# Clearing an output in quarter blocks, spread over the loads of a recurrence and expert kernel

## Chip, cores and metric

One core of a Trainium2 chip. The metric is the device time of one execution in microseconds (us); lower is better.

## What is computed

Two stages, the second on the output of the first:

```python
# x, f_logit: (4, 5056, 256) float32; lower_bound: (256,)
f = lower_bound + (1 - lower_bound) * sigmoid(f_logit)
h[t] = f[t] * h[t-1] + (1 - f[t]) * x[t]          # along the 5056 steps, y[:, t] = h[t]

x = y.reshape(20224, 256)                         # N = 20224 tokens, D = 256, E = 8, F = 1024
logits = x @ w_gate
expert = argmax(logits); gate_w = softmax(logits)[expert]
out = zeros((20224, 256))
for e in range(8):
    tok = the up to 80 tokens of expert e with the largest gate_w
    out[tok] = gate_w[tok] * (relu(x[tok] @ w1[e]) @ w2[e])
```

At most 640 of the 20224 rows of the output are other than zero, and the kernel has to write all of them: 20.7 MB of zeros.

## The kernel before

The sequence is cut into 40 units (`n_unit`): 10 groups of 512 steps (the last one of 448) by 4 sequences. A unit is worked in a pipeline. `load` (lines 195 to 202) brings f and x of a unit from DRAM to two tiles of 128 rows (112 in the last group), with four buffers each. `gate` (L206, ScalarE) makes the sigmoid in place, `enter` (L210, GpSimd) multiplies it into x, `to_channels` (L217, TensorE) transposes both, the sigmoid to `sp` and the product to `up`, eight transposes each; `decay` (L228, ScalarE) writes the factors to `h_all`, and `scan` (L234, VectorE) runs the recurrence there. `logits` (L246, TensorE) multiplies the unit by the gate weights into `lg`. With each finished group, copies, transposes and small VectorE work pick the candidates of each expert (L253 to L351).

The loop (lines 385 to 402) runs n from -3 to 39 and issues in each step the load of unit n + 3, the gate and product of unit n + 2, the transposes of n + 1, the scan of n and the logits of n - 1. All loads, all clears of the output and all expert weights are DMAs issued by SyncE (SP), in the order of the code; an instruction there that waits holds up all that stand behind it. A load waits until its buffer is free, which is when TensorE has transposed the unit four before. Apart from that, SyncE's DMAs share eight completion counters in turn, so each waits until the one eight before it has landed.

Zeros: GpSimd fills a small tile (L173), and ScalarE's queue copies it several times over to a block in DRAM, `z_dram`, 128 rows of 2048 numbers, 1.05 MB (L175, in `setup`). A clear (L146) is a DMA of this block to 8 of the 158 rows that each of 128 stripes of the output has; 20 clears cover it, the last of 6 rows. Before the loop's last load five have gone out; where they go out is written in the loop (L396: behind the logits of the steps n = -3, 5, 13, 21, 29 and 37), behind the first three weights (L445, eleven), and in the experts behind w1 of expert 2 and w2 of expert 1 (L652, the other three):

```python
            if n % 8 == 5:
                clear_some(1)
...
    clear_some(11)
...
                if e == 0 and not again:
                    clear_some(len(zeros))
```

After the loop come the rest of the choice, the selection (L485 to L556, VectorE for the most part), and the eight experts: `gather` (L583, three engines copy 80 columns), `hidden` (L601, TensorE), `relu` (L609), `result` (L616, TensorE), `finish` (L622) and `scatter` (L625, an indirect DMA of GpSimd, which may not pass a clear). Weights come in halves of 0.524 MB (L433 for w1, L437 for w2) to seven buffers, whose place in memory the loop's tiles hold until the loop is through.

Of the kernel before, what the change touches and what calls it, by code (L numbers as in the profile page):

```python
# [17 lines left out]
P = 128  # L18
# [5 lines left out]
def kernel(  # L24
# [11 lines left out]
    nc = tc.nc  # L36
    B, S, D = x.shape
    E, _, F = w1.shape
# [3 lines left out]
    R = 4  # L42
    G = P * R
    n_grp = (S + G - 1) // G
    n_unit = n_grp * B
# [93 lines left out]
    z_dram = dram.tile([P, ZR * D], F32, name="z_dram")  # L139
    out_z = out.rearrange("(p k) d -> p (k d)", p=P)  # L140
    clears = range(0, N // P, ZR)
    zeros = list(clears)

    def clear(k):
        n = min(ZR, N // P - k) * D
        nc.sync.dma_start(out=out_z[:, ds(k * D, n)], in_=z_dram[:, :n])  # L146

    def clear_some(m):
        for k in zeros[:m]:
            clear(k)  # L150
        del zeros[:m]

    with tc.tile_pool(name="ld", bufs=4) as ld, \
         tc.tile_pool(name="gsm", bufs=1) as gsm, \
# [57 lines left out]
        def to_channels(n, src, dst, pool, tag):  # L212
            k = run(n // B)
            for o in range(DC):
                ps = pool.tile([P, G], F32, name=tag, tag=tag)
                for r in range(R):
                    nc.tensor.transpose(ps[:, ds(r * k, k)], src[n][:, r, ds(o * P, P)],  # L217
                                        ident[:k, :k])
                dst[n, o] = ps[:, :R * k]
            del src[n]  # L220
# [29 lines left out]
        def aside(g):  # L250
            k = run(g)
            lss[g] = gsm.tile([P, B * P], F32, name="ls", tag="ls")[:, :B * k]
            nc.scalar.copy(lss[g].rearrange("p (b t) -> p b t", b=B), lgs.pop(g)[:, :, :k])  # L253
# [111 lines left out]
        def unit(f, m):  # L365
            if 0 <= m < n_unit:
                f(m)


        AHEAD = 3  # L370
        of_group, of_batch = [], []

        def chosen(g):
            choice(g)
            if g in batches:
                of_batch.extend(work(*batches[g]))

        def some_of(jobs, k):
            while jobs and k:
                for f in jobs.pop(0):  # L380
                    f()
                k -= 1

        setup()
        for n in range(-AHEAD, n_unit):
            unit(load, n + AHEAD)
            unit(gate, n + 2)
            unit(enter, n + 2)
            unit(lambda m: to_channels(m, sts, sps, pss, "sp"), n + 1)
            unit(lambda m: to_channels(m, uts, ups, psu, "up"), n + 1)  # L390
            unit(decay, n + 1)
            unit(scan, n)
            some_of(of_group, 1)
            some_of(of_batch, 1 if n < n_unit - 2 else 2)
            unit(logits, n - 1)
            if n % 8 == 5:  # L396
                clear_some(1)
            if n > 0 and n % B == 0:
                g = n // B - 1
                of_group += [[lambda g=g: aside(g)], [lambda g=g: shifted(g)],  # L400
                             [lambda g=g: chosen(g)]]
# [40 lines left out]
    w_sb = {}  # L442
    for key in order[:3]:
        w_sb[key] = weights(*key)
    clear_some(11)  # L445


    def tokens(pool, at, ids):
# [115 lines left out]
    def experts(again):  # L564
        with tc.tile_pool(name="xp", bufs=2) as xp, \
             tc.tile_pool(name="mp", bufs=2) as mp, \
             tc.tile_pool(name="psd", bufs=1, space=PSUM) as psd, \
             tc.tile_pool(name="psh", bufs=4, space=PSUM) as psh, \
             tc.tile_pool(name="psy", bufs=2, space=PSUM) as psy:
            w = {} if again else w_sb  # L570
            late = list(order if again else order[3:])
            X, XT, HID, Y = {}, {}, {}, {}


            def gather(e):
                X[e] = xp.tile([P, DC, K], F32, name="xe", tag="xe")
                k = 0
                for engine, copy, n in ways:
                    _, at_tok = nc.values_load_multi_w_load_instructions(
                        trow[ds(e, 1), ds(k, n)], engines=(engine,), min_val=0, max_val=N - 1,  # L580
                        skip_runtime_bounds_check_because="token numbers come from iota")
                    for j, v in enumerate(at_tok):
                        copy(X[e][:, :, ds(k + j, 1)], h_all[:, :, ds(v, 1)])  # L583
                    k += n

            def scaled(e):
                XT[e] = mp.tile([P, DC, K], F32, name="xt", tag="xt")
                x_e = X.pop(e)
                for o in range(DC):
                    nc.vector.tensor_scalar_mul(XT[e][:, o], x_e[:, o], omlb[:, ds(o, 1)])  # L590

            def hidden(e):
                HID[e] = mp.tile([P, FC, K], F32, name="hid", tag="hid")
                xt = XT.pop(e)
                halves = w.pop((1, e))
                ps = []
                for i in range(2):
                    h_ps = psh.tile([P, CH, K], F32, name="h_ps", tag="h_ps")
                    for c in range(CH):
                        for o in range(DC):  # L600
                            nc.tensor.matmul(h_ps[:, c], halves[i][:, o, ds(c * P, P)], xt[:, o],  # L601
                                             start=o == 0, stop=o == DC - 1,
                                             skip_group_check=True)
                    ps.append(h_ps)
                return ps

            def relu(e, ps):
                for i in range(2):
                    nc.scalar.activation(HID[e][:, ds(i * CH, CH)], ps[i], ACT.Relu)  # L609

            def result(e):
                y_ps = psy.tile([K, D], F32, name="y_ps", tag="y_ps")
                halves = w.pop((2, e))
                hid = HID.pop(e)
                for c in range(FC):
                    nc.tensor.matmul(y_ps, hid[:, c], halves[c // CH][:, c % CH],  # L616
                                     start=c == 0, stop=c == FC - 1)
                return y_ps

            def finish(e, y_ps):  # L620
                Y[e] = mp.tile([K, D], F32, name="y", tag="y", bufs=3)
                nc.vector.tensor_scalar_mul(Y[e], y_ps, gsl[:, ds(e, 1)])  # L622

            def scatter(e):
                nc.gpsimd.indirect_dma_start(  # L625
                    out=out, out_offset=bass.IndirectOffsetOnAxis(ap=goal[:, ds(e, 1)], axis=0),
                    in_=Y.pop(e), in_offset=None, bounds_check=N - 1, oob_is_err=False)

            def more(m):
                for key in late[:m]:  # L630
                    w[key] = weights(*key)
                del late[:m]

            if again:
                more(3)
            for e in range(2):
                gather(e)
                scaled(e)
            ps = hidden(0)
            relu(0, ps)  # L640
            more(1)
            if not again:
                total = psd.tile([1, 4], F32, name="total")
                nc.tensor.matmul(total, ones, doubts[:, :4], start=True, stop=True)
            for e in range(E):
                if e + 2 < E:
                    gather(e + 2)
                if e + 1 < E:
                    ps = hidden(e + 1)
                    relu(e + 1, ps)  # L650
                    more(1)
                if e == 0 and not again:  # L652
                    clear_some(len(zeros))
                y_ps = result(e)
                more(1)
                if e + 2 < E:
                    scaled(e + 2)
                finish(e, y_ps)
                if e > 0:
                    scatter(e - 1)  # L660
                if e == 1 and not again:
                    found = consts.tile([1, 1], F32, name="found")
                    nc.vector.tensor_reduce(found, total, AX.X, ALU.add)
                    nc.vector.tensor_copy(doubt, found)
            scatter(E - 1)

    experts(False)


    unsure = nc.values_load(doubt, min_val=0, max_val=4 * P,  # L670
                            skip_runtime_bounds_check_because="a sum of 4 * P flags")
    with tc.If(unsure > 0):
        with tc.tile_pool(name="all", bufs=1) as sel, \
# [34 lines left out]
            for e in range(E):  # L708
                nc.gpsimd.indirect_dma_start(
                    out=tok[:, ds(e, 1)], out_offset=None, in_=id_list,  # L710
# [7 lines left out]
            for k in clears:  # L718
                clear(k)
        experts(True)  # L720
    hpool.release()

# [30 lines left out]
```

## Time and profile before

| what | us |
|---|---|
| median of three runs | 262.97 (261.96 to 263.56) |
| the profiled execution, its own time | 263.93 |
| its span, first to last instruction | 262.0 |
| busy: TensorE, VectorE, GpSimd, ScalarE | 202.5, 169.4, 135.6, 134.1 |
| loop, selection, experts | to about 150, to about 190, to the end |

Times in the trace are counted from the start of the span. The rows name the engines PE (TensorE), DVE (VectorE), ACT (ScalarE), POOL (GpSimd) and SP (SyncE); SPq and ACTq are the queues on which SyncE and ScalarE issue DMAs, and a row there is the issue, not the transfer. A busy share is an average over stages with different limits: a stage is read from what its last waits were for.

### The profile page before, as it was taken

To read this page: it belongs to the slowest core of one execution; us is meant where nothing else is said; L and a number is where in the kernel's file an instruction comes from. 1 tells how busy PE (TensorE), PEld (TensorE's weight loads), DVE (VectorE), ACT (ScalarE), POOL (GpSimd) and SP (SyncE) were. 2 spreads that over 40 slices of the span, in tenths; PEclk is the share of its full clock that TensorE was granted. 3 is DMA by queue.
4 is the path that set the end of the run, shared out by engine and by line. 5 is a ranking of instruction groups with operands and counts; after the bars stand their busy time and mean duration, and the time that the engine had idled before them with its cause. 6 is when DMAs were issued, how large, how long until landed. Compare 5 with 4: busy or idle time off the path is not lost.

```text
span 262.0 us, 5950 instructions
## 1 busy us (share of the span) xinstructions
PE 202.5 (77%) x1755; PEld 158.2 (60%) x1755; DVE 169.4 (65%) x484; ACT 134.1 (51%) x390; POOL 135.6 (52%) x275
## 2 busy tenths in 40 slices
PE   0519989799999789999899941117099999999990
PEld 0417767576767567776577720016099788888860
DVE  0627877869696779698769687982565066656200
ACT  3037875867777957676977530000445424555100
POOL 2318775868686569694596510300575025664111
PEclk9999999999999999999979995555555699999997
DMA  6699999999999998999999199999994999999700
GB/s 172 249 335 385 383 404 369 386 365 362 381 384 350 356 353 273 362 324 377 316 241 287 65 360 409 345 309 315 324 300 152 393 292 392 390 333 315 233 18 21
DMA packets 58904, 81.09 MB, mean 309 GB/s; under 512 B 2800, under 2 KB 51568, under 8 KB 56432
## 3 DMA queue, kind: packets, MB, share of 16 engines
q1 hardware_dynamic: 57408, 78.91, 89.7%
q10 hardware_dynamic: 1072, 1.06, 1.1%
q0 software_dynamic: 384, 0.66, 0.7%
q8 instruction: 16, 0.26, 0.4%
q14 instruction: 24, 0.20, 0.3%
HBM read 78.91 MB, written 22.41 MB: 387 GB/s over the span
## 4 chain that ended last, share of the span: by engine, by line
PE 52%; DMA 18%; DVE 8%; issue 6%; ACT 6%; POOL 6%; SPq 2%; POOLq 0%; DVEq 0%; ACTq 0%
PE h_ps L601 12%; PE lg L246 10%; PE sp L217 9%; PE up L217 9%; PE y_ps L616 8%; DMA x_t<-in_x_dram 7%; POOL x_t L210 5%; DMA w_sb<-in_moe_w_dram 5%; DMA out_dram<-z_dram 4%; DVE beat L513 3%; ACT h_all L228 3%; DMA z_dram<-zero 3%; DVE h_all L234 2%; PE flat_p L536 2%; PE lt L261 1%
## 5 line engine op out<-in xcount | busy, mean ns | idle before, releaser
L210 POOL TENSOR_TENSOR x_t<-f_t,x_t 128x1024 f32<-128x1024 f32 (+1 forms) x40 | 94.9, 2376 | 47.2 <-DMA x_t<-in_x_dram 21.5
L234 DVE TENSOR_TENSOR_SCAN h_all<-h_all,up 128x512 f32<-128x512 f32 (+1 forms) x80 | 95.5, 1241 | 14.8 <-ACT h_all L228 11.4
L228 ACT ACTIVATE h_all<-sp,nomlb 128x512 f32<-128x512 f32 (+1 forms) x80 | 49.9, 676 | 16.0 <-PE sp L217 15.9
L217 PE MATMUL sp<-ident,f_t 128*128 128x128 f32 (+1 forms) x320 | 45.8, 288 | 15.9 <-ACT h_all L228 8.9
L217 PEld LDWEIGHTS sp<-ident,f_t 128*128 128x128 f32 (+1 forms) x320 | 35.9, 146 | 32.9 <-issue 19.4
L206 ACT ACTIVATE f_t<-f_t 128x1024 f32<-128x1024 f32 (+1 forms) x40 | 42.6, 1064 | 17.7 <-DMA f_t<-in_f_logit_dram 17.7
L217 PE MATMUL up<-ident,x_t 128*128 128x128 f32 (+1 forms) x320 | 44.5, 284 | 4.7 <-POOL x_t L210 3.8
L246 PE MATMUL lg<-h_all,wg 128*32 128x128 f32 (+1 forms) x640 | 43.5, 401 | 5.1 <-ACT ls L253 3.6
L601 PE MATMUL h_ps<-xt,w_sb 128*128 128x80 f32 x256 | 36.4, 311 | 7.2 <-issue 7.0
L217 PEld LDWEIGHTS up<-ident,x_t 128*128 128x128 f32 (+1 forms) x320 | 37.6, 147 | 7.1 <-POOL x_t L210 5.6
L583 ACT COPY xe<-h_all 128x2 f32 x224 | 22.2, 190 | 37.6 <-issue 32.2
L601 PEld LDWEIGHTS h_ps<-xt,w_sb 128*128 128x128 f32 x256 | 36.1, 227 | 8.2 <-issue 7.1
L583 DVE COPY xe<-h_all 128x2 f32 x224 | 26.5, 177 | 14.8 <-issue 14.8
L583 POOL COPY xe<-h_all 128x2 f32 x192 | 24.3, 195 | 15.4 <-DVE goal L475 8.5
L616 PE MATMUL y_ps<-w_sb,hid 128*80 128x256 f32 x128 | 30.3, 393 | 0.0
L246 PEld LDWEIGHTS lg<-h_all,wg 128*32 128x32 f32 x640 | 18.2, 119 | 18.0 <-ACT ls L253 5.5
L625 POOL DMA_INDIRECT out_dram<-y,goal x8 | 7.5, 940 | 33.3 <-DVE y L622 15.6
L616 PEld LDWEIGHTS y_ps<-w_sb,hid 128*80 128x80 f32 x128 | 19.5, 157 | 8.2 <-issue 1.2
L609 ACT ACTIVATE hid<-h_ps 128x320 f32<-128x320 f32 x16 | 7.0, 436 | 22.9 <-PE h_ps L601 19.6
L622 DVE TENSOR_SCALAR y<-y_ps,gsl 80x256 f32<-80x256 f32 x8 | 3.8, 480 | 21.0 <-PE y_ps L616 21.0
L284 DVE TENSOR_REDUCE mx<-lt 128x16 f32<-128x128 f32 (+1 forms) x10 | 2.9, 290 | 12.7 <-PE lt L261 12.6
L286 ACT COPY shift<-lt 128x128 f32<-128x128 f32 (+1 forms) x10 | 2.7, 266 | 15.8 <-DVE lt L285 15.8
(103 smaller groups left out, 102.8 us busy)
## 6 DMA issues: line engine op xcount, KB each, us to landing
out_dram<-z_dram SPq DMA_DIRECT2D x19, 1024.0 KB, 10.0
f_t<-in_f_logit_dram SPq DMA_DIRECT2D x36, 512.0 KB, 7.0
x_t<-in_x_dram SPq DMA_DIRECT2D x36, 512.0 KB, 6.6
w_sb<-in_moe_w_dram SPq DMA_DIRECT2D x32, 512.0 KB, 5.8
f_t<-in_f_logit_dram SPq DMA_DIRECT2D x4, 448.0 KB, 8.2
x_t<-in_x_dram SPq DMA_DIRECT2D x4, 448.0 KB, 7.3
z_dram<-zero ACTq DMA_DIRECT2D x1, 1024.0 KB, 7.5
out_dram<-z_dram SPq DMA_DIRECT2D x1, 768.0 KB, 10.3
```

What stands on the lines that cost most here:

```text
L206: nc.scalar.activation(s_t, s_t, ACT.Sigmoid, scale=-1.0)
L210: nc.gpsimd.tensor_tensor(u_t, sts[n], u_t, ALU.mult)
L217: nc.tensor.transpose(ps[:, ds(r * k, k)], src[n][:, r, ds(o * P, P)], ident[:k, :k])
L228: nc.scalar.activation(columns(n, o), sps.pop((n, o)), ACT.Identity, scale=nomlb[:, ds(o, 1)], bias=1.0)
L234: nc.vector.tensor_tensor_scan(h, h, ups.pop((n, o)), h_all[:, o, ds(spot(n) - 1, 1)] if n >= B else 0.0, ALU.mult, ALU.add)
L246: nc.tensor.matmul(lgs[g][ds(r * LC, LC), b, :k], wg[:, o], columns(n, o)[:, r::R], start=o == 0, stop=o == DC - 1, skip_group_check=True)
L513: nc.vector.tensor_scalar(beat, rivals, vals[:, ds(k, 1)], 0.0, ALU.is_gt, ALU.add, accum_out=rank[:, ds(k, 1)])
L583: copy(X[e][:, :, ds(k + j, 1)], h_all[:, :, ds(v, 1)])
L601: nc.tensor.matmul(h_ps[:, c], halves[i][:, o, ds(c * P, P)], xt[:, o], start=o == 0, stop=o == DC - 1, skip_group_check=True)
L609: nc.scalar.activation(HID[e][:, ds(i * CH, CH)], ps[i], ACT.Relu)
L616: nc.tensor.matmul(y_ps, hid[:, c], halves[c // CH][:, c % CH], start=c == 0, stop=c == FC - 1)
L625: nc.gpsimd.indirect_dma_start(out=out, out_offset=bass.IndirectOffsetOnAxis(ap=goal[:, ds(e, 1)], axis=0), in_=Y.pop(e), in_offset=None, ...
```

## The change

A clear may now take a quarter of the block, 32 of the 128 rows, 0.262 MB, and the list of clears is a list of quarters. In the loop one quarter goes out in each step from n = 8 to 35, and twelve in the step n = 36, in which the last unit's load goes out; the clears that the loop had at n = -3, 5, 13, 21, 29 and 37 are gone. Ten blocks stand for 40 quarters by then. The other ten, in whole blocks, follow the first three weights; the clears among the experts' weights are gone.

```diff
-    zeros = list(clears)
-
-    def clear(k):
+    QP = P // R
+    zeros = [(k, q) for k in clears for q in range(R)]
+
+
+    def clear(k, q=None):
         n = min(ZR, N // P - k) * D
-        nc.sync.dma_start(out=out_z[:, ds(k * D, n)], in_=z_dram[:, :n])
+        rows = slice(0, P) if q is None else ds(q * QP, QP)
+        nc.sync.dma_start(out=out_z[rows, ds(k * D, n)], in_=z_dram[rows, :n])
 
     def clear_some(m):
-        for k in zeros[:m]:
+        for k, q in zeros[:m]:
+            clear(k, q)
+        del zeros[:m]
+
+    def clear_rest():
+        clear_some(len(zeros) % R)
+        for k, _ in zeros[::R]:
             clear(k)
-        del zeros[:m]
+        zeros.clear()
...
-            if n % 8 == 5:
+            if n + AHEAD == n_unit - 1:
+                clear_some(3 * R)
+            elif 2 * B <= n < n_unit - AHEAD:
                 clear_some(1)
...
-    clear_some(11)
+    clear_rest()
...
-                if e == 0 and not again:
-                    clear_some(len(zeros))
```

Only SyncE's order moves. Its first instructions before, where `f_t` and `x_t` are a unit's two loads and `out_dram<-z_dram` is a clear:

```order
L198 DMA f_t<-in_f_logit_dram 128x4x256
L201 DMA x_t<-in_x_dram 128x4x256
L146 DMA out_dram<-z_dram 128x2048
L198 DMA f_t<-in_f_logit_dram 128x4x256
L201 DMA x_t<-in_x_dram 128x4x256
L198 DMA f_t<-in_f_logit_dram 128x4x256
L201 DMA x_t<-in_x_dram 128x4x256
```

The same place now:

```order
L207 DMA f_t<-in_f_logit_dram 128x4x256
L210 DMA x_t<-in_x_dram 128x4x256
L207 DMA f_t<-in_f_logit_dram 128x4x256
L210 DMA x_t<-in_x_dram 128x4x256
L207 DMA f_t<-in_f_logit_dram 128x4x256
L210 DMA x_t<-in_x_dram 128x4x256
```

The clear between the loads of units 0 and 1 is gone; the first zeros now follow the load of unit 11. From there to the last load one quarter stands between the loads of any two units. The end of the loop before, from the load of the last unit to the experts' first weights:

```order
L198 DMA f_t<-in_f_logit_dram 112x4x256
L201 DMA x_t<-in_x_dram 112x4x256
L146 DMA out_dram<-z_dram 128x2048
L433 DMA w_sb<-in_moe_w_dram 128x2x512 x4
L437 DMA w_sb<-in_moe_w_dram 128x4x256 x2
L146 DMA out_dram<-z_dram 128x2048 x11
L433 DMA w_sb<-in_moe_w_dram 128x2x512 x2
L437 DMA w_sb<-in_moe_w_dram 128x4x256 x2
L146 DMA out_dram<-z_dram 128x2048 x2
L146 DMA out_dram<-z_dram 128x1536
L433 DMA w_sb<-in_moe_w_dram 128x2x512 x2
```

The same place now, from the load of the unit before the last:

```order
L207 DMA f_t<-in_f_logit_dram 112x4x256
L210 DMA x_t<-in_x_dram 112x4x256
L149 DMA out_dram<-z_dram 32x2048
L207 DMA f_t<-in_f_logit_dram 112x4x256
L210 DMA x_t<-in_x_dram 112x4x256
L149 DMA out_dram<-z_dram 32x2048 x12
L444 DMA w_sb<-in_moe_w_dram 128x2x512 x4
L448 DMA w_sb<-in_moe_w_dram 128x4x256 x2
L149 DMA out_dram<-z_dram 128x2048 x9
L149 DMA out_dram<-z_dram 128x1536
L444 DMA w_sb<-in_moe_w_dram 128x2x512 x2
```

Between the last load and the first weights stand three blocks' worth of zeros where one was, behind the first weights ten blocks where eleven were, and none further on.

## Rows read from the trace of the kernel before

**Rows 1.** Page, part 2: DMA busy tenths, GB/s in 40 slices

```profile
DMA  6699999999999998999999199999994999999700
...
GB/s 172 249 335 385 383 404 369 386 365 362 381 384 350 356 353 273 362 324 377 316 241 287 65 360 409 345 309 315 324 300 152 393 292 392 390 333 315 233 18 21
```

**Rows 2.** Timeline of SyncE's DMA issues at the start: start us, us, instruction

```profile
1.21 0.49 SPq L201 DMA_DIRECT2D x_t<-in_x_dram  x1
...
9.78 0.61 SPq L146 DMA_DIRECT2D out_dram<-z_dram  x1
...
10.43 0.58 SPq L198 DMA_DIRECT2D f_t<-in_f_logit_dram  x1
```

**Rows 3.** SyncE's waits: who waited for whom, us in total, times, longest

```profile
SPq L146 <- DMA z_dram<-zero: 8.1, 1, 8.1
```

**Rows 4.** Timeline of other engines at the start; brackets: idle time, releaser

```profile
2.28 0.58 ACTq L175 DMA_DIRECT2D z_dram<-zero  x1
...
7.36 2.35 POOL L210 TENSOR_TENSOR x_t<-f_t,x_t 128x1024 f32<-128x1024 f32 x1 [4.92 <-DMA x_t<-in_x_dram]
...
16.67 1.06 ACT L206 ACTIVATE f_t<-f_t 128x1024 f32<-128x1024 f32 x1 [9.85 <-DMA f_t<-in_f_logit_dram]
...
18.47 2.35 POOL L210 TENSOR_TENSOR x_t<-f_t,x_t 128x1024 f32<-128x1024 f32 x1 [8.76 <-DMA x_t<-in_x_dram]
...
20.88 1.97 PE L217 MATMUL up<-ident,x_t 128*128 128x128 f32 x8 [0.56 <-POOL x_t L210]
```

**Rows 5.** Start by stretch: us, busy by engine, then PEclk, DMA share, GB/s

```profile
2.00:4.00 2.00, 0.00 (x0) 0.00 (x0) 0.00 (x0) 1.11 (x1) 0.44 (x2) 1.00 0.76 158
...
4.00:6.00 2.00, 0.00 (x0) 0.00 (x0) 0.24 (x2) 0.42 (x2) 0.00 (x0) 1.00 0.92 286
...
8.00:10.00 2.00, 1.14 (x6) 0.73 (x5) 1.97 (x3) 0.00 (x0) 1.71 (x1) 1.00 0.50 195
```

**Rows 6.** Stretches of the loop, its end and the selection, columns as above

```profile
32.80:45.60 12.80, 12.09 (x130) 8.62 (x128) 9.33 (x13) 8.38 (x13) 8.03 (x4) 1.00 1.07 387
...
112.00:114.00 2.00, 2.00 (x26) 1.26 (x24) 1.93 (x6) 1.39 (x3) 2.00 (x2) 1.00 0.89 218
...
130.00:140.00 10.00, 8.83 (x79) 6.92 (x80) 7.12 (x9) 7.11 (x12) 7.73 (x5) 0.83 1.10 240
...
148.00:150.00 2.00, 2.00 (x20) 1.91 (x19) 0.27 (x1) 1.16 (x2) 0.00 (x0) 1.00 0.00 0
...
166.00:182.00 16.00, 4.83 (x33) 4.78 (x34) 10.75 (x41) 0.00 (x0) 2.83 (x11) 0.50 0.98 319
```

**Rows 7.** Timeline of TensorE in the loop: three lg groups and the last up

```profile
37.56 1.10 PE L246 MATMUL lg<-h_all,wg 128*32 128x128 f32 x16 [0.44 <-ACT ls L253]
...
51.68 1.10 PE L246 MATMUL lg<-h_all,wg 128*32 128x128 f32 x16 [0.52 <-ACT ls L253]
...
64.46 1.11 PE L246 MATMUL lg<-h_all,wg 128*32 128x128 f32 x16 [0.52 <-ACT ls L253]
...
148.68 0.93 PE L217 MATMUL up<-ident,x_t 112*128 112x112 f32 x8
```

**Rows 8.** Timeline at the end of the loop, SyncE and GpSimd

```profile
137.53 0.31 SPq L201 DMA_DIRECT2D x_t<-in_x_dram  x1
...
145.48 2.37 POOL L210 TENSOR_TENSOR x_t<-f_t,x_t 112x1024 f32<-112x1024 f32 x1
...
149.68 1.92 SPq L433 DMA_DIRECT2D w_sb<-in_moe_w_dram  x4
```

**Rows 9.** Tile x_t, issues from 137 to 138 us: issue to landing

```profile
DMA to landing us min/median/max: 7.3/7.3/7.3
```

**Rows 10.** Tile x_t, all issues: issue to landing

```profile
DMA to landing us min/median/max: 4.9/6.7/10.1
```

**Rows 11.** Timeline of TensorE, experts: first and fourth hidden layer

```profile
190.33 7.09 PE L601 MATMUL h_ps<-xt,w_sb 128*128 128x80 f32 x32 [7.01 <-issue]
...
216.70 3.77 PE L601 MATMUL h_ps<-xt,w_sb 128*128 128x80 f32 x32 [0.20 <-DMA w_sb<-in_moe_w_dram]
```

## Prediction

> **What bounds the kernel now.** I read the page's slices first [rows 1]: the DMA engines are near full for most of the span, with two holes: the first two slices (13 us, 172 and 249 GB/s) and the 23rd, 144 to 151 us (65 GB/s). Then SyncE's own timeline and waits [rows 2, 3], since every load, clear and weight goes through that one queue; then what the other engines waited for at the start [rows 4], bandwidth by stretch [rows 5, 6], and the pace of TensorE in the loop [rows 7].
>
> The first hole: SyncE issues the load of x for unit 0 at 1.21 us and nothing more until 9.78, because the next instruction is a clear, and that waits 8.1 us for the block of zeros to be written to DRAM [rows 2, 3]. Unit 1's loads stand behind it. So ScalarE sits idle 9.85 us until f of unit 1 has landed, GpSimd 8.76 us until x has, and TensorE's second group of `up` starts at 20.88 [rows 4]. Meanwhile the DMA engines fall to 195 GB/s in 8 to 10 us [rows 5].
>
> From there TensorE sets the pace. The `lg` group that follows the copy of a finished group's logits starts at 51.68 and at 64.46, four units later: 12.78 us, 3.20 us a unit [rows 7]. A unit's two loads are 2 x 0.524 = 1.049 MB, which at the 387 GB/s of the stretch 32.8 to 45.6 [rows 6] is 2.71 us: under the pace, so loads can run ahead. The four units before that took 51.68 - 37.56 = 14.12 us [rows 7]; a clear of 1.05 MB had gone out among their loads, and 1.3 us were lost.
>
> The last four units' loads are dearer: 112 rows, 0.917 MB a unit, and the stretch 130 to 140 ran at 240 GB/s with a full DMA share [rows 6], 3.82 us a unit. The last x goes out at 137.53 and lands 7.3 us later, at 144.8 [rows 8, 9]; GpSimd takes it at 145.48, TensorE transposes it at 148.68, and the weights, whose buffers lie where the loop's were, go out at 149.68 [rows 7, 8]. That is the second hole: 0 GB/s from 148 to 150 [rows 6], after one clear. Behind it the selection and the experts form one chain to the end.
>
> **The change part by part.**
>
> *No clear before unit 1's loads.* Its wait of 8.1 us and issue go; six loads leave back to back. How much earlier x of unit 1 lands: by 6 us some 2 x 0.158 + 2 x 0.286 = 0.89 MB had moved [rows 5], and that part stays. If the zeros' copy (1.05 MB, issued by ScalarE at 2.28 [rows 4]) goes wholly ahead, 4 x 0.524 + 1.05 = 3.15 MB must move, the remaining 2.26 MB at 387 GB/s in 5.8 us: 11.8. If it comes last, 1.21 MB: 9.1. The landing of the last byte adds between 0 and 1 us: of f and x of unit 0 alone 0.16 MB were still to come at 6 us, so 6.4 at 387 GB/s at the earliest, and x had landed by 7.36 [rows 4]. I take the late end and 0.5: 12.3. GpSimd started on that x at 18.47 [rows 4]: 6.2 us earlier, and `up` follows at 14.7. Bounds: 8.7 us (the time from SyncE's issue at 1.21 to that of unit 1 at 10.43, less an issue of 0.5 [rows 2]) and 1.5 us (the 2.26 MB at 213 GB/s, the mean of the three stretches of rows 5: 16.6, with the landing 17.1).
>
> *Clears in quarters.* 5 of before's 6 loop clears go out before the last load, 1.05 MB at once each; now 28 quarters of 0.262 MB, one a unit from unit 8 on, 7.34 MB instead of 5.24. The stall of 1.3 us between 37.56 and 51.68 has no clear behind it any more: the first quarter follows the load of unit 11. I count -1.3 us (bounds 0 and -2). What the quarters cost the DMA engines: at the mixed rate 387 GB/s 0.68 us each; at the 319 GB/s of clears alone (166 to 182) 0.82; at the worst two microseconds with a clear in flight, 218 GB/s (112 to 114), 1.20 [all rows 6]. I take 0.68, since it is the row where a clear runs among queued loads, as here. Then a unit asks for 2.71 + 0.68 = 3.39 us of DMA against 3.20 of TensorE: so loads that ran ahead before unit 11 lose 0.2 us of their lead with each unit, and TensorE feels nothing until it is gone.
>
> [...]
>
> *When the last x lands.* If the DMA engines never idle, all that is ahead of it sets the time: 1.05 (zeros) + 36 x 1.049 + 7.34 = 46.1 MB; less 0.89, 45.3 MB at 387 GB/s is 117 us from 6: 123; 3.67 MB at 240 GB/s, 15.3: 138.3; with 0.5 for the landing 138.8. TensorE's chain, moved by 6.2 + 1.3 = 7.5 us, would want it picked up at 145.48 - 7.5 = 138.0. So DMA is the later of the two by 0.8 us, and the end of the loop comes 145.48 - 138.8 = 6.7 us earlier.
>
> *Twelve quarters behind the last load.* SyncE's next instructions are the weights, which waited until 149.68 anyway [rows 8] and now would go out at 143. 3.15 MB are 8.1 us at 387 GB/s, 139 to 147, of which 4 us fill the hole; the weights end some 4 us later than with an empty queue. Nothing needs them for long: the first hidden layer stood at 190.33 [rows 11], now near 183. Cost 0; without that cover it would be 4 us.
>
> *9.75 blocks behind the first weights, none in the experts.* 10.2 MB instead of 11.5, still in the selection's stretch at 319 GB/s, 32 us: ending near 188; the weights queued behind are first needed by the third hidden layer, two layers of 7.09 us [rows 11] after 183. The three clears taken from among the experts' weights had cost TensorE one wait of 0.20 us [rows 11]: -0.2, bounds 0 and -1. GpSimd's first scatter, which has to wait for all zeros, no longer stands behind late ones; TensorE does not wait for it.
>
> Sum: 6.7 + 0.2 = 6.9 us. The profiled execution's 263.93 becomes 257.0. It is 0.96 above the median of the three runs, 262.97, on which the forecast stands: 256.1.
>
> **The rivals.**
>
> *The start gives all that SyncE waited.* `up` of unit 1 comes 8.7 us earlier and DMA keeps up (quarters hide in slack): 262.97 - 8.7 - 1.3 - 0.2 = 252.8. For it: loads now queue deeper early on, where the share was 0.76 and 0.92 with few in flight [rows 5]. Against: the last loads' 240 GB/s.
>
> *The start gives less.* The first loads move no faster than the 286 GB/s of 4 to 6 us [rows 5], beside the zeros' copy: 2.26 MB in 7.9 us, x at 14.4, 4.1 us earlier: 262.97 - 4.1 - 1.3 - 0.2 = 257.4.
>
> *The quarters eat the gain.* At 0.82 us each, 28 x 0.14 = 3.9 us later than 138.8: 142.7, picked up at once against 145.48: 2.8 + 0.2 gained, 260.0. For it: the clear-only rate is what the DMA engines do when reading and writing DRAM [rows 6].
>
> *Slower: the loop becomes DMA-bound.* If a quarter among loads costs 1.20 us, the last x lands at 138.8 + 28 x 0.52 = 153.4, 7.9 us later than it was picked up before, and all else follows: 262.97 + 7.9 - 0.2 = 270.7. It decides from 0.68 + 6.9/28 = 0.93 us a quarter (no gain); from 1.02 us it is 1% slower. For it: 218 GB/s was seen; against it: that stretch had a DMA share of 0.89, so the engines were not full [rows 6]. [...]
>
> That the change doesn't do what it says can't be seen: the order rows show all zeros, once each, and no instruction of another engine moved.
>
> **How the numbers follow.** Forecast 0.60 (own range 253 to 259), full start 0.12, smaller start 0.10, quarters eat it 0.12, slower 0.06. About 1%, 2.6 us, is what a measurement of this kernel can tell from no change: faster means under 260.3. The first three cases lie there, and nearly half of the fourth, less a little for the forecast's own spread: 0.83. Same 0.11, slower 0.06. Range 251.5 to 261: from a little under the full start to just past the fourth case; what it leaves out is the slower rival and the edges.
>
> **What would show it.** Right: SyncE issues six loads before 5 us; `up` of unit 1 near 14.7; no wait of SyncE on the zeros' copy; some 380 GB/s from 40 to 120 us; the last x landing near 139 with GpSimd waiting for it; weights issued near 143; no DMA gap before them; experts spaced as before. Wrong: `up` of unit 1 after 17; GpSimd or ScalarE waiting on loads through the middle of the loop (quarters dearer than 0.9 us); weights issued after 146; a hidden layer waiting for weights.

## The result, and the profile after

The changed kernel took 254.56 us (median of 4 runs, 254.13 to 255.03) against 263.25 (4 runs, 261.96 to 263.56) beside it: a ratio of 0.9679, 95% interval 0.9641 to 0.9717, 8.7 us or 3.2% faster. The profiled execution took 254.13 us with a span of 252.2; before's took 263.93 with 262.0. Forecast were 256.1 us and a gain of 6.9.

The page's slices of the changed kernel (6.3 us each), against [rows 1]:

```profile
DMA  6999999999999999999999999999954599999700
GB/s 176 382 386 384 384 382 394 390 390 391 395 386 391 392 390 392 393 391 389 318 313 360 304 380 408 347 321 318 295 184 148 187 276 312 318 305 306 241 18 21
```

Both holes are gone: the second slice holds 382 GB/s instead of 249, and where 65 stood the slices now hold 360 and 304. SyncE's issues at the start, of the changed kernel, against [rows 2]:

```profile
1.20 0.50 SPq L210 DMA_DIRECT2D x_t<-in_x_dram  x1
1.74 0.51 SPq L207 DMA_DIRECT2D f_t<-in_f_logit_dram  x1
2.29 0.81 SPq L210 DMA_DIRECT2D x_t<-in_x_dram  x1
3.14 0.77 SPq L207 DMA_DIRECT2D f_t<-in_f_logit_dram  x1
3.95 1.50 SPq L210 DMA_DIRECT2D x_t<-in_x_dram  x1
```

With the first f at 0.72, six loads go out by 3.95 us, and the wait of [rows 3] no longer exists. The other engines at the start, against [rows 4]: ScalarE's queue and ScalarE, GpSimd, TensorE, each in order of time.

```profile
5.04 0.58 ACTq L184 DMA_DIRECT2D z_dram<-zero  x1
5.66 1.28 ACT L215 ACT_TABLE_LOAD   x1 [5.66 <-DVE nomlb L178]
6.95 1.06 ACT L215 ACTIVATE f_t<-f_t 128x1024 f32<-128x1024 f32 x1
...
8.09 4.67 POOL L219 TENSOR_TENSOR x_t<-f_t,x_t 128x1024 f32<-128x1024 f32 x2 [5.65 <-ACT f_t L215]
15.18 2.35 POOL L219 TENSOR_TENSOR x_t<-f_t,x_t 128x1024 f32<-128x1024 f32 x1 [2.42 <-DMA x_t<-in_x_dram]
...
10.50 1.97 PE L226 MATMUL up<-ident,x_t 128*128 128x128 f32 x8 [0.41 <-POOL x_t L219]
13.78 0.60 PE L226 MATMUL up<-ident,x_t 128*128 128x128 f32 x4
14.94 0.66 PE L226 MATMUL up<-ident,x_t 128*128 128x128 f32 x4 [0.56 <-DVE h_all L243]
17.59 1.09 PE L226 MATMUL up<-ident,x_t 128*128 128x128 f32 x8 [1.07 <-POOL x_t L219]
```

The row of the kernel before that answers to the last of these, `up` of unit 2:

```profile
23.83 1.09 PE L217 MATMUL up<-ident,x_t 128*128 128x128 f32 x8
```

Two things there were not foreseen. The copy of the zeros, which no line of the change touches, goes out at 5.04 us instead of 2.28, and ScalarE's first work stands behind it. And GpSimd now waits 2.42 us for the x of unit 2, whose load shares the DMA engines with that copy. Still, `up` of unit 2 starts at 17.59, 6.24 us earlier than in the kernel before.

TensorE's groups that answer to [rows 7], and the end of the loop on SyncE and GpSimd, against [rows 8]:

```profile
30.98 1.09 PE L255 MATMUL lg<-h_all,wg 128*32 128x128 f32 x16 [0.39 <-ACT ls L262]
...
43.75 1.10 PE L255 MATMUL lg<-h_all,wg 128*32 128x128 f32 x16 [0.52 <-ACT ls L262]
...
56.53 1.10 PE L255 MATMUL lg<-h_all,wg 128*32 128x128 f32 x16 [0.52 <-ACT ls L262]
...
140.71 0.93 PE L226 MATMUL up<-ident,x_t 112*128 112x112 f32 x8
...
129.55 0.31 SPq L210 DMA_DIRECT2D x_t<-in_x_dram  x1
129.91 10.84 SPq L149 DMA_DIRECT2D out_dram<-z_dram  x12
141.70 2.43 SPq L444 DMA_DIRECT2D w_sb<-in_moe_w_dram  x4
...
134.81 2.39 POOL L219 TENSOR_TENSOR x_t<-f_t,x_t 112x1024 f32<-112x1024 f32 x1
137.16 0.41 POOL L333 TENSOR_TENSOR gm<-oh,gt 128x128 f32<-128x128 bf16 x1
137.52 2.36 POOL L219 TENSOR_TENSOR x_t<-f_t,x_t 112x1024 f32<-112x1024 f32 x1
```

Subtracting row by row from before tells where the time went: the three `lg` groups stand 6.58, 7.93 and 7.93 us earlier and the last `up` 7.97. So the start gave 6.2 to 6.6, the stretch of before's stall another 1.35 (both groups now 12.77 us apart, where 14.12 stood), and from there to the end of the loop nothing was gained or lost. GpSimd takes the last x at 137.52, right behind its operation before, with no wait for a transfer. The transfer's own row (tile `x_t`, issues from 129 to 130 us):

```profile
DMA to landing us min/median/max: 7.2/7.2/7.2
```

So the last x, issued at 129.55, landed at 136.8, 0.8 us before it was taken.

Bandwidth by stretch of the changed kernel (columns as in [rows 5]), against [rows 6]: the middle of the loop with quarters among its loads, and the last units' loads with theirs.

```profile
33.00:120.00 87.00, 81.64 (x870) 61.22 (x869) 72.40 (x94) 65.89 (x96) 62.77 (x31) 1.00 1.08 391
120.00:136.00 16.00, 13.60 (x147) 9.64 (x149) 12.38 (x17) 12.60 (x19) 11.69 (x8) 1.00 1.09 315
```

391 GB/s answers to the 387 on which the price of a quarter rested; the 315 of the second row, against 240, contradicts a step of the prediction. The work of the 130 to 140 us of [rows 6] lies 8 us earlier now, as the loop does, at 122 to 132. Two rows from there:

```profile
124.00:128.00 4.00, 3.29 (x35) 2.48 (x36) 1.83 (x3) 3.18 (x6) 3.83 (x4) 1.00 1.09 314
128.00:132.00 4.00, 3.50 (x39) 2.56 (x38) 3.90 (x6) 2.02 (x5) 2.03 (x2) 1.00 1.09 310
```

Over the whole ten us it is 312 GB/s. 72 more than 240 are 0.72 MB, about the three quarters (0.79 MB) that now ride in such a stretch, and the loop didn't lengthen for them: from an `lg` group ahead of this stretch to one behind it are 27.84 us before (119.10 to 146.94) and 27.76 after (111.21 to 138.97), with TensorE's granted clock at 0.83 and 1.00 within the stretch. In the experts, against [rows 11]:

```profile
196.16 4.47 PE L627 MATMUL y_ps<-w_sb,hid 128*80 128x256 f32 x16
200.47 3.69 PE L612 MATMUL h_ps<-xt,w_sb 128*128 128x80 f32 x32
...
207.46 3.69 PE L612 MATMUL h_ps<-xt,w_sb 128*128 128x80 f32 x32
```

The fourth hidden layer no longer waits for its weights. From the first hidden layer (182.11, before 190.33) to the last `y` (238.94, before 248.25) the chain is 56.83 us instead of 57.92: another 1.1. The two profiled executions lie 9.8 us apart, the medians 8.7: 8.0 of the 9.8 are in the loop, 1.1 here, and 0.7 between them and at the very end.

### The profile page after: what moved, and what is told of

Read it like the earlier page. It is cut to its first block, busy times and chain, and to the rows that moved or that the text cites. A ratio compares the mean times of both kernels' runs of the same rounds, so it can differ in the third digit from the quotient of the medians.

```text
span 252.2 us, 5978 instructions
## 1 busy us (share of the span) xinstructions
PE 198.6 (79%) x1755; PEld 155.6 (62%) x1755; DVE 171.5 (68%) x484; ACT 134.3 (53%) x390; POOL 135.5 (54%) x275
## 3 DMA queue, kind: packets, MB, share of 16 engines
q10 hardware_dynamic: 1072, 1.06, 1.2%
## 4 chain that ended last, share of the span: by engine, by line
PE 56%; DMA 10%; DVE 9%; issue 8%; ACT 7%; POOL 4%; SPq 3%; POOLq 0%; DVEq 0%; ACTq 0%
PE h_ps L612 14%; PE y_ps L627 11%; PE lg L255 10%; PE sp L226 9%; PE up L226 7%; DMA x_t<-in_x_dram 4%; POOL x_t L219 4%; ACT h_all L237 4%; DVE beat L524 3%; DMA out_dram<-z_dram 3%; DMA f_t<-in_f_logit_dram 3%; DVE h_all L243 2%; PE flat_p L547 2%; PE lt L270 2%; ACT ls L262 1%
## 5 line engine op out<-in xcount | busy, mean ns | idle before, releaser
L226 PE MATMUL sp<-ident,f_t 128*128 128x128 f32 (+1 forms) x320 | 45.0, 285 | 10.4 <-ACT f_t L215 8.2
L226 PE MATMUL up<-ident,x_t 128*128 128x128 f32 (+1 forms) x320 | 43.1, 277 | 4.7 <-POOL x_t L219 2.7
L226 PEld LDWEIGHTS up<-ident,x_t 128*128 128x128 f32 (+1 forms) x320 | 36.2, 143 | 7.0 <-POOL x_t L219 4.1
L594 DVE COPY xe<-h_all 128x2 f32 x224 | 26.6, 180 | 14.7 <-issue 14.7
L627 PE MATMUL y_ps<-w_sb,hid 128*80 128x256 f32 x128 | 29.6, 387 | 0.0
L293 DVE TENSOR_REDUCE mx<-lt 128x16 f32<-128x128 f32 (+1 forms) x10 | 2.9, 291 | 12.5 <-PE lt L270 12.3
```

## The experiments

The ratio of each is to the kernel before, timed beside it on the same chip.

**The changed kernel once more** (c1).

> The changed kernel itself, as the measure for the runs beside it: 254 to 255.5 us.

254.83 us (254.29 to 255.31), ratio 0.9669 [0.9624, 0.9713]. Its last `up` stands at 140.84, and its experts' chain is 57.25 us (182.49 to 239.74): that chain alone differs by 0.4 us between two profiles of one kernel.

**The start alone** (e1): the kernel before, without its clear ahead of unit 1.

```diff
-            if n % 8 == 5:
+            if n > 0 and n % 8 == 5:
...
-    clear_some(11)
+    clear_some(12)
```

> The kernel before, but its first clear (between the loads of units 0 and 1) goes out behind the first weights instead, so twelve there; all other clears whole and where they were. If the first loads' wait is the gain: up of unit 2 near 17.6 us instead of 23.83, the weights out 6 to 8 us earlier than 149.68, 255 to 257.5 us. Rival, the gain lies in the quarters or in the zeros behind the last load: at most 3 us of it here, 260 us or more.

256.52 us (255.91 to 256.79), ratio 0.9732 [0.9688, 0.9775]: this one edit gives 6.7 us of the 8.4 to 8.7. `up` of unit 2 stands at 17.89, the last `up` at 141.63, 7.05 earlier than before. The fourth hidden layer still waits for its weights:

```profile
209.46 3.77 PE L601 MATMUL h_ps<-xt,w_sb 128*128 128x80 f32 x32 [0.26 <-DMA w_sb<-in_moe_w_dram]
```

**All but the start** (e2): the changed kernel with one whole block put back ahead of unit 1's loads.

```diff
-            if n + AHEAD == n_unit - 1:
+            if n == -AHEAD:
+                clear(zeros[0][0])
+                del zeros[:R]
+            elif n + AHEAD == n_unit - 1:
```

> The changed kernel with one whole block between the loads of units 0 and 1 again, quarters and twelve as changed, nine blocks behind the weights. If the first loads' wait is the gain: the loop ends 6 to 7 us later than in the changed kernel, 260.5 to 262 us. Rival, the gain lies in the quarters or the twelve: 257 us or less.

262.01 us (260.95 to 262.54, 10 runs), ratio 0.9949 [0.9923, 0.9976]: 1.3 us faster than before, and 7.2 slower than the repeat beside it. SyncE's rows show the wait back: the block goes out at 9.91, unit 1's loads behind it.

```profile
9.91 0.60 SPq L149 DMA_DIRECT2D out_dram<-z_dram  x1
10.56 0.58 SPq L207 DMA_DIRECT2D f_t<-in_f_logit_dram  x1
```

The two halves, 6.7 and 1.3, add to 8.0 of 8.4 to 8.7: there is little interplay. The last `up` is 1.46 us earlier than before, so these 1.3 us come out of the loop: the two `lg` groups that stood 14.12 us apart stand 12.78 apart here (37.51 and 50.29), with the start as it was and no clear among their loads. In e1, where that clear still goes out, they stand 13.50 apart (31.21 and 44.71).

**Whole blocks in place of quarters** (e3): the same bytes, a block with every fourth unit and three behind the last load.

```diff
-            if n + AHEAD == n_unit - 1:
-                clear_some(3 * R)
-            elif 2 * B <= n < n_unit - AHEAD:
-                clear_some(1)
+            if n + AHEAD == n_unit - 1 or 2 * B <= n < n_unit - AHEAD and n % R == R - 1:
+                for k, _ in zeros[:(3 if n + AHEAD == n_unit - 1 else 1) * R:R]:
+                    clear(k)
...
```

> The changed kernel with whole blocks in place of quarters: one every fourth step of the loop from n = 11 to 35, three behind the last load; the same bytes by the same steps. If TensorE paces the loop and loads have a lead of several us: within 1 us of the changed kernel. Rival, a block of 1.05 MB among the loads costs 1.3 us of stall as it did in before: seven of them, some 9 us, 263 us; if only those without lead, 256 to 259.

256.44 us (255.07 to 257.91), ratio 0.9743 [0.9679, 0.9806], and a last `up` at 141.47. Against the repeat beside it that is 1.6 us of medians and 0.6 us in the profile's loop, with intervals that overlap: quarters are not worse than blocks, and perhaps a little better. The rate from 33 to 120 us is 386 GB/s against 391: in this pair of runs whole blocks of 1.05 MB moved no more bytes per second than quarters. The pair is no test of what either could reach, since TensorE paced both; e6 below has quarters at 396 GB/s where DMA sets the pace, and no run has whole blocks there.

**Without the twelve** (e4): nothing behind the last load, 13 whole blocks less a quarter behind the weights.

```diff
-            if n + AHEAD == n_unit - 1:
-                clear_some(3 * R)
-            elif 2 * B <= n < n_unit - AHEAD:
+            if 2 * B <= n < n_unit - AHEAD - 1:
                 clear_some(1)
```

> The changed kernel without the twelve quarters behind the last load; thirteen blocks behind the first weights instead of ten. If the zeros there only fill time in which nothing waits for DMA: within 0.7 us of the changed kernel, the DMA engines idle for some 2 us before the weights. Rival, they keep the zeros from reaching the experts: weights of the third hidden layer late, 2 us or more slower.

254.54 us (254.31 to 254.97), ratio 0.9655 [0.9617, 0.9694]: no difference. The stretch of 138 to 146 us falls from the changed kernel's 317 GB/s (first row) to 132 (second), and nothing behind it comes later.

```profile
138.00:146.00 8.00, 6.06 (x86) 4.10 (x87) 5.97 (x11) 4.04 (x7) 1.89 (x1) 1.00 0.91 317
```
```profile
138.00:146.00 8.00, 6.08 (x83) 4.07 (x81) 5.98 (x11) 4.16 (x8) 2.00 (x1) 1.00 0.39 132
```

So the second hole of [rows 1] was a hole in the DMA engines' work, and no cost.

**Three blocks among the experts again** (e5).

```diff
-        for k, _ in zeros[::R]:
+        for k, _ in zeros[:-3 * R:R]:
...
+                if e == 0 and not again:
+                    for k, _ in zeros[::R]:
+                        clear(k)
+                    zeros.clear()
                 y_ps = result(e)
```

> The changed kernel, but the last three blocks go out among the experts' weights again, seven behind the first weights. If that was the wait of 0.2 us and little else: 0.2 to 0.6 us slower than the changed kernel. Rival, the late zeros held up more (the first scatter, GpSimd's gathers): 1.5 us or more.

256.1 us (254.24 to 257.28), ratio 0.9724 [0.9679, 0.9769], an interval that overlaps the changed kernel's. The profile, taken in the fastest of its four runs (254.24), has the wait back and wider than before:

```profile
207.36 3.77 PE L612 MATMUL h_ps<-xt,w_sb 128*128 128x80 f32 x32 [0.43 <-DMA w_sb<-in_moe_w_dram]
```

From the third to the fourth hidden layer (199.78 to 207.36) it takes 7.58 us, against 6.99 in the changed kernel: 0.6 us. By the medians the three cost 1.2 us against the changed kernel and 1.6 against e4 beside it; what goes beyond 0.6 isn't settled.

**Two quarters with each unit** (e6), to reach the point where DMA sets the pace: 56 ahead of the last load in place of 28 (the expectation miscounted them as 50 and 25).

```diff
             elif 2 * B <= n < n_unit - AHEAD:
-                clear_some(1)
+                clear_some(2)
```

> Two quarters ride with each of the 25 units from the twelfth on, fifty in place of twenty-five, and the rest behind the last loads as far as they go. Theory (a quarter takes the queues some 0.65 us among the loads, and one a unit fits under TensorE's 3.20 us a unit): a unit's loads are then 2.7 us of DMA time and its two quarters 1.3, so the loop goes at some 4.0 us a unit until the last load, some 15 us later than TensorE would get there; the loop's last matmul of the gate falls from 140.7 to 153 to 157 us and the run takes 266 to 272 us, with part of it given back behind the loop, where fewer blocks are left. Rival (a quarter is nearly free wherever it rides, as it came out among the 112-row loads): the loop ends within 2 us of the changed kernel's and the run takes 254 to 257 us.

270.84 us (269.75 to 271.82), ratio 1.0269 [1.0231, 1.0306]. The last `up` falls to 156.38, 15.7 us later than in the changed kernel, while the DMA engines run at 396 GB/s throughout:

```profile
48.00:136.00 88.00, 73.11 (x748) 53.55 (x741) 65.18 (x82) 60.21 (x85) 54.20 (x27) 0.98 1.07 396
```

At that rate (0.396 MB a us) 28 more quarters are 28 x 0.262 / 0.396 = 18.5 us. 15.7 of it show; the other 2.8 would be what the changed kernel's loads were still ahead of TensorE. TensorE is busy for 73.1 of 88 us here; in the changed kernel's middle it is busy for 81.6 of 87. The slower rival was a mechanism that exists, and one quarter a unit stays under it.

**Three quarters in each gap between the last four units' loads** (e7), six fewer behind.

```diff
-                clear_some(3 * R)
+                clear_some(6)
             elif 2 * B <= n < n_unit - AHEAD:
-                clear_some(1)
+                clear_some(3 if n >= n_unit - AHEAD - B else 1)
```

> The changed kernel with three quarters instead of one in each of the three gaps between the last four units' loads, and six instead of twelve behind the last load. If the 112-row loads leave the DMA engines room that zeros use: GB/s of 120 to 136 us up from 315 to 370 or more, the last x landing as soon after its issue (7.7 us) within 1.5 us, time within 1 us. Rival, each of the six costs 0.68 us of the queue there: the last x some 4 us later, 2 to 4 us slower.

258.41 us (257.17 to 259.43), ratio 0.9809 [0.9755, 0.9863]: some 3.7 us slower than the changed kernel. The DMA engines carry 363 GB/s from 120 to 136 us, more than 315, but the last two units' loads leave later, since SyncE is held in the quarters:

```profile
122.41 3.20 SPq L149 DMA_DIRECT2D out_dram<-z_dram  x3
125.90 0.33 SPq L207 DMA_DIRECT2D f_t<-in_f_logit_dram  x1
126.36 0.41 SPq L210 DMA_DIRECT2D x_t<-in_x_dram  x1
127.01 3.48 SPq L149 DMA_DIRECT2D out_dram<-z_dram  x3
131.29 0.32 SPq L207 DMA_DIRECT2D f_t<-in_f_logit_dram  x1
```

The last f goes out at 131.29 instead of 128.00, and the last `up` at 142.45 instead of 140.71. So there is room among the 112-row loads, for one quarter a unit and not for three; 1.7 us of the loss are in the profile's loop (an execution of 257.17), and the rest is spread behind it.

**The copy of the zeros later** (e8): ScalarE issues it behind its third sigmoid, so that neither the first sigmoid nor unit 2's x stands behind it.

```diff
-            m = ZR * D // ZC
-            nc.scalar.dma_start(out=z_dram.rearrange("p (m z) -> p m z", m=m),
-                                in_=zero.unsqueeze(1).broadcast_to([P, m, ZC]))
...
             unit(gate, n + 2)
+            if n == 0:
+                m = ZR * D // ZC
+                nc.scalar.dma_start(out=z_dram.rearrange("p (m z) -> p m z", m=m),
...
```

> The changed kernel, but the copy of the zeros to DRAM is issued by ScalarE in step n = 0 instead of before the first load's sigmoid. If that copy's wait (its issue at 5.04 us, for a completion counter that it shares with the first small load) and its bytes are what is left at the start: sigmoid of unit 0 near 5.7 instead of 6.95, up of unit 2 near 15.5 instead of 17.59, 1.5 to 2.5 us faster than the changed kernel. Rival, the first loads' own bandwidth sets it: within 0.5 us.

259.28 us (258.81 to 260.41), ratio 0.9836 [0.9788, 0.9883]: 4.5 us slower than the changed kernel, though the first `up` comes at 9.55 instead of 10.50. VectorE's and GpSimd's rows say why:

```profile
7.11 2.39 POOL L217 TENSOR_TENSOR x_t<-f_t,x_t 128x1024 f32<-128x1024 f32 x1 [4.67 <-DMA x_t<-in_x_dram]
...
7.26 0.14 DVE L190 TENSOR_SCALAR row_i<-row_i 128x1 int32<-128x1 int32 x1
7.44 2.08 DVE L192 CAST row_f<-row_i 128x3 f32<-128x3 int32 x1
...
9.73 2.40 POOL L217 TENSOR_TENSOR x_t<-f_t,x_t 128x1024 f32<-128x1024 f32 x1 [0.24 <-DMA x_t<-in_x_dram]
9.83 2.34 DVE L195 TENSOR_SCALAR mine<-col_f,row_f 128x8 f32<-128x8 f32 x1
...
12.50 2.36 POOL L217 TENSOR_TENSOR x_t<-f_t,x_t 128x1024 f32<-128x1024 f32 x1 [0.36 <-DMA x_t<-in_x_dram]
12.53 2.41 DVE L198 CAST col_f<-col_i 128x128 f32<-128x128 int32 x1
...
15.18 2.34 POOL L217 TENSOR_TENSOR x_t<-f_t,x_t 128x1024 f32<-128x1024 f32 x1 [0.32 <-DMA x_t<-in_x_dram]
15.30 2.37 DVE L200 TENSOR_TENSOR before<-before,mates 128x128 f32<-128x128 f32 x1
17.59 3.43 DVE L241 TENSOR_TENSOR_SCAN h_all<-h_all,up 128x512 f32<-128x512 f32 x3
```

VectorE builds its constants just ahead of its first scan. Four operations that take 0.23 to 0.54 us where no product runs (e9) take 2.1 to 2.4 here: each starts beside one of GpSimd's products and ends within 0.2 us of its end (9.50, 12.13, 14.86 and 17.52), and the first scan waits until 17.59. The row at 7.26 ran beside the first product and wasn't held, so it isn't every operation; what holds the others no run here shows beyond these times. That the held constants are what costs the time, e10 below bears out: of the 4.1 us by which the last `up` is late here (144.84), 0.3 are left when the constants alone are moved. In the changed kernel two operations are hit (8.12 to 10.54 and 10.45 to 12.84, beside two products from 8.09 to 12.76) and the first scan starts at 13.67.

**The constants first** (e9): VectorE's constants moved ahead of its two operations on the lower bound, into the time in which it waits for that load.

> The changed kernel with VectorE's constants (rows and columns shifted, place, mine, before, mates) ahead of its products with the lower bound, in the time in which it waits for that load. Theory (they take 2.4 us each only where they stand beside GpSimd's product, and hold the first scan to 13.67): each takes 0.15 to 0.3 us, the first scan starts at 11 to 12.5 us, the second unit's matmuls lose their wait of 0.56 us; the third unit still waits for its x, so the run gains 0 to 1 us: 253.5 to 255 us. Rival (the constants are slow for another reason, or hold nothing): they still take 2 us or the time stays within 0.3 us of the changed kernel's.

254.86 us (253.75 to 255.61), ratio 0.9662 [0.9628, 0.9697]. All of them are done by 4.33 us at 0.14 to 0.54 us each, and the first scan starts at 11.82. But `up` of unit 2 stays at 17.71 and the last one at 140.88: in the changed kernel the constants hid behind unit 2's x.

**Both** (e10): the constants first and the copy later.

> The constants first, and the copy of the zeros issued by ScalarE behind its first sigmoids, so that it neither waits for the first small load nor lies ahead of the third unit's x. Theory (the copy's new place holds ScalarE and the x of unit 2, and the constants alone made the later copy slower): the first sigmoid starts near 5.3 us, the first scan near 10, the third unit's matmuls at 15 to 16.5 us in place of 17.6, and the run gains 1 to 2.5 us on the changed kernel: 252 to 253.5 us. Rival (the DMA queues bound the start whatever the order): the third unit's matmuls stay at 17 us or later and the run is within 0.5 us of the changed kernel's 254.6.

255.09 us (254.35 to 256.27), ratio 0.9686 [0.9657, 0.9716]: the rival. `up` of unit 2 is at 15.81, 1.8 us earlier, as hoped; then GpSimd waits for unit 4's x, with the copy's megabyte now ahead of it, and the last `up` stands at 141.04.

```profile
15.59 2.39 POOL L218 TENSOR_TENSOR x_t<-f_t,x_t 128x1024 f32<-128x1024 f32 x1 [0.38 <-DMA x_t<-in_x_dram]
20.91 2.35 POOL L218 TENSOR_TENSOR x_t<-f_t,x_t 128x1024 f32<-128x1024 f32 x1 [2.93 <-DMA x_t<-in_x_dram]
```

**No copy at all** (e11): the constants first, and the clears read a tile of 256 zeros a partition in SBUF, whole blocks eight times over.

```diff
-    ZC = 512
-    z_dram = dram.tile([P, ZR * D], F32, name="z_dram")
+    ZC = 256
+    zero = consts.tile([P, ZC], F32, name="zero")
...
-        nc.sync.dma_start(out=out_z[rows, ds(k * D, n)], in_=z_dram[rows, :n])
...
+        else:
+            nc.sync.dma_start(out=out_z[:, ds(k * D + q * (n // R), n // R)].rearrange("p (m z) -> p m z", z=ZC),
+                              in_=zero.unsqueeze(1).broadcast_to([P, n // R // ZC, ZC]))
...
```

> The constants first, and no z_dram at all: the clears read a 128 x 256 tile of zeros in SBUF (a quarter is a stripe of 2 KB in each of the 128 partitions of out, in place of 8 KB in 32 of them), so the copy of 1 MB at the start and ScalarE's hold behind it are gone, not moved. Theory (the copy's 2.6 us of DMA time is what bounds the start wherever it is put): the third unit's matmuls start at 15.5 to 16.5 us as with the later copy, unit 5's x comes without a wait of over 0.5 us, the last up falls 1 to 2.5 us before the changed kernel's 140.7, and the run takes 252 to 254 us. Rival (a unit's loads and TensorE's work are so close that the lead is lost again before the clears begin, or clears out of SBUF go slower than those out of DRAM): the last up within 0.7 us of 140.7, or the DMA rate under 370 GB/s while quarters ride, and 254 us or more.

257.45 us (256.35 to 257.87), ratio 0.9776 [0.9749, 0.9803]: slower than the changed kernel by 2.6 to 2.9, though the start does what the theory wanted. `up` of unit 2 comes at 14.92 and the last one at 139.29, 1.4 us earlier than the changed kernel's. The loss stands behind the loop. GpSimd's copies of the chosen tokens, which in the changed kernel began at 176.77 within a microsecond of their destinations (`goal`, done at 175.81), begin 5.5 us behind them here (`goal` at 174.57):

```profile
180.09 3.06 POOL L596 COPY xe<-h_all 128x2 f32 x24 [13.00 <-issue]
```

ScalarE's and VectorE's begin within 0.4 us of it, all three put down to "issue", and the DMA rate falls just then, from 305 GB/s (179 to 180) and 287 (180 to 181) to 75 (181 to 182): the traffic ends about a microsecond after the engines start. What holds the three engines this trace doesn't show; it stays open.

## Why the prediction was right, point by point

**The start.** The size was right, the path was not. Foreseen was 6.2 us by the x of unit 1 (`up` at 14.7); it came at 13.78, with its second half at 14.94, and unit 2's `up` was 6.24 earlier. Undone it costs 7.2 us, alone it gives 6.7. That 6.2 and 6.24 agree is luck, since another unit's load and another transfer decide it. (The step's lower bound, 18.47 less 17.1, is 1.4 and not 1.5.) That the x of unit 1 lands at 12.3 was too late a guess: GpSimd had it right behind unit 0's product. What holds the start instead is the copy of the zeros. It went out at 2.28 us before [rows 4]; in the changed kernel ScalarE's queue has a wait at the copy's line (L184, `EVENT_SEMAPHORE`, 17 ns, at 4.98), which the trace of the kernel before has not.

The completion counters are semaphores in the records of both traces: the transfers of SyncE's and ScalarE's queues together, not SyncE's alone as said ahead of the prediction, signal eight of them in turn. Of the pairs of transfers that stand eight apart, signal the same one and have the landing of the first on record (46 before, 95 after), none has the second issued before that landing. With six loads in front instead of two, the copy comes round to semaphore 100, which the first small load (`lb`) signals (before, the copy had 105, which no transfer ahead of it signals), and the wait at L184 is for 100: VectorE, which waits for the same load, starts at 4.98, and the copy goes out at 5.04. Its packets run from 9.2 to 13.6 us (5.9 to 9.4 before). It then delays unit 2's x, for which GpSimd waits 2.42 us, and e10 and e11 show that this is the bound of the start: moved, its megabyte costs the same a little later; taken away, unit 2 starts 2.7 us earlier and the last `up` 1.4 (e11). The constants, which both move too, do neither by themselves (e9).

**The stall of 1.3 us.** Right: 14.12 us became 12.77, and in e2, with the start as before, 12.78: it was the clear.

**A quarter at 0.68 us among the loads.** Right: 391 GB/s (0.67 us), though at a pace that TensorE sets; in e6, where two a unit leave no lead and DMA sets the pace, loads and quarters pass at 396 (0.66 us). No run here times a quarter by itself, with no other transfer beside it. The rival "the quarters eat the gain" has no row for it.

**DMA later than TensorE by 0.8 us at the last x.** This step failed. It took the 240 GB/s of 130 to 140 us [rows 6] for all that the DMA engines could do with 112-row loads, since their busy share was 1.10, and put the quarters on top: 3.82 + 0.68 = 4.50 us a unit. A unit with its quarter is 0.917 + 0.262 = 1.18 MB, and at the measured 315 GB/s that takes 3.74 us, less than the unit alone was priced at. In the same ten us of the loop's work the rate rose from 240 to 312 GB/s with the quarters, at shares of 1.10 and 1.09, and in e7 the stretch of 120 to 136 us ran at 363 with a lower share, 1.06. A share over 1 did not mean that no more bytes could pass. So the last x landed 0.8 us ahead of TensorE's chain instead of 0.8 behind it, and that chain stayed the bound.

The loop ended 8.0 us earlier instead of 6.7. Of these 1.3 us 0.8 lie in this step and 0.5 in the chain itself, which moved by 7.97 us where 6.2 + 1.3 = 7.5 had been summed. The rival "the start gives all that SyncE waited" was right in this part (DMA keeps up) and wrong in the other: the start gave 6.2 to 6.6 us and not 8.7. The measured 254.56 lies halfway between it (252.8) and the forecast (256.1).

**The twelve at no cost.** Right (e4), and for the reason given.

**The experts, 0.2 us.** Undersized, but by less than the chain says, which is 1.1 us shorter in one profile (just past the bound of 1) and 0.7 in the other. From the third to the fourth hidden layer 0.36 us went (7.35 us in the kernel before, 6.99 after, in both profiles), the wait of [rows 11] and what it cost around it; e5 and e1, which still clear there, have 7.58 and 7.40. Most of the rest lies in the first `y` group (4.47 and 4.90 us in the two profiles of the changed kernel, 5.14 before). The granted clock, at 0.50 through the two hidden layers before it, rises to 1.00 within this group: 1.7, 2.6 and 3.1 us after its start, in this order, read in stretches of one us. What sets that moment no run here shows. It moves between two profiles of one kernel, and e7, which has no clears among the experts, has 5.14 too: this part isn't the change's.

Of the signs named: six loads before 5 us, `up` of unit 1 near 14.7 (13.78 and 14.94), no wait on the copy, 391 GB/s, experts without a wait for weights came as said. GpSimd waiting for the last x near 139 didn't, nor did weights near 143 (141.70), both through the step that failed.

## What to carry to other kernels

Here a transfer that waited 8.1 us [rows 3] held every load behind it on its queue: of all the clears that the change moves, the one that was moved out from ahead of unit 1's loads gave three quarters of the gain. Spread writes cost their bytes at the rate of the row where they rode among loads (396 GB/s in e6, 0.66 us a quarter), and nothing while the loads kept a lead (two `lg` groups stand 12.78 us apart from 43.75 to 56.53 with a quarter a unit, and 12.79 in the kernel before from 64.46 to 77.25, in which no clear goes out); price the second one a unit before adding it (here 16 us). A rate read where another engine set the pace was no limit, however full the busy share looked: 240 GB/s at a share of 1.10 became 312 at 1.09.

## What the runs showed that was not expected

- An unchanged transfer moved by 2.8 us (2.28 to 5.04) because with six loads ahead of it instead of two it signals the same semaphore as the first small load, and waited for that one: a wait that no line of the source shows.
- Small VectorE operations took 2.1 to 2.4 us beside GpSimd's product, so that work released earlier (e8) cost 4.5 us.
- The DMA engines' share was 1.06 to 1.10 at 240, 315, 363 and 391 GB/s alike.
- In the kernel whose clears read SBUF (e11) three engines started 5.5 us after their destinations were ready, against 1.0 in the changed kernel; the cause is open.
